# Where VectorE's weight conversions stand among the block products of a two-layer MLP, one Trainium2 core

## The chip, the core and the metric

The kernel runs on one core of a Trainium2 chip. Its time is device microseconds of one execution. TensorE (PE in the rows) multiplies, VectorE (DVE), ScalarE (ACT) and GpSimd (POOL) work on its results, SyncE (SP) issues the transfers. Each engine runs its instructions in the order in which the program lists them: an instruction that waits holds up all that stand behind it on that engine.

## The reference

Clustered attention gives `x` (2 batches, 768 tokens, 512 features). Two MLPs follow:

```python
X = np.fft.fft(np.fft.fft(x, axis=1), axis=2)
u = x + np.real(X)
un = (u - u.mean(-1)) / sqrt(var(u) + 1e-6)
u = u + np.maximum(un @ w_ch1, 0.0) @ w_ch2          # 512 -> 2048 -> 512
h = np.maximum(u @ w_in, 0.0)                        # 512 -> 1024
conv_out = 3-tap convolution of h along the tokens with conv_w
out = (h * sigmoid(conv_out)) @ w_out                # 1024 -> 512
```

The weights come as 64-bit floats. A conversion on the chip makes them 32-bit, and each is then multiplied as two 16-bit parts, high and low.

## The kernel before, in words

Attention comes first, and the change does not touch it. Then the first MLP runs over batch 0 (`g = 0`) and batch 1 (`g = 1`), sixteen blocks of 128 hidden features each (`f`), and after it the second MLP over both batches, eight blocks each.

**The products of a pair.** For batch 1 the up-projection of two blocks `2p` and `2p+1`, called pair p here, is made of seven block products instead of eight, in `ups(p)`. TensorE makes them in the order p1, p6, p2, p7, p5, p4, p3; each is six matmuls of 384 columns. What comes out is added up on VectorE:

- `u1` is a copy of p1 by ScalarE; `u2 = u1 + p6`; `u3 = u2 + p7`;
- `c1` low half `= u1 + p2`; `c2` high half `= u3 + p5`; `c2` low half `= u3 + p4`;
- p5 is also copied by ScalarE, and GpSimd makes `u4 = u2 + p5`; `c1` high half `= u4 + p3`;
- `keep` makes the hidden block from `c2`, then from `c1`: ScalarE the high part (L1754), VectorE the low part (L1755).

Every product lies in one of **two banks** of tag `up`, taken in turn. So TensorE can start a product only when all readers of the product two before it are done. The transposed token tiles and the token scales (`xT`, `cb`, below) take their turn in the same two banks.

**The down-projection between them.** `downs` is a generator: each step is the three matmuls of 512 columns of one token tile, here called a tile. `in_turn` deals products (u) and tiles (d) by a string; a pair has seven products and the twelve tiles of two blocks: `u d u d d u d u d d` in the even block, then `u d d u d d u d d`. After the tiles named in `when`, a step of `side` runs. For batch 1 that is `gate_in(0)`, which prepares batch 0 for the second MLP: two steps that measure tokens, six that turn a token tile (four transposes on TensorE into a bank, then a copy by ScalarE, L1906, and the low part by VectorE, L1907), two that spread the scales (`cb`).

**Sums of weights.** Four of the seven products take sums of weight blocks. `weight_sums(p)` makes them on GpSimd (L1719 to L1723, tile `sv`, one buffer), then splits them: high part by ScalarE (L1726), low part by VectorE (L1727).

**Conversions of the second MLP's weights.** `load_w("b", i)` loads 1 MB into one of two raw buffers and converts it: VectorE L710, L711, L713 (`wb`), ScalarE the square of the low word L712, a check L716, and two sums of squares L759, whose scratch is the raw buffer, so that it is free for the next load only behind them. The eight loads stand in the code behind blocks 1, 3, 5, 7, 9, 10, 11, 12 of batch 1. A scheduler then orders each engine's queue: it may take an instruction from further down in the code when it reckons that it is ready. `tc.issue_after(i)` makes it keep the instructions under it behind `i` on the same engine.

At the end of the stage `scales("b")` adds the sums of squares on TensorE (`sumsb`), and `split_16` splits converted weights (L1681 ScalarE, L1682 VectorE) while the second MLP's first products (`u`, L492) run.

Of the kernel before, what the change touches and what calls it, by code (L numbers as in the profile page):

```python
# [449 lines left out]
def tile_net(ctx, tc, qk, v, cen, w12, w34, conv, dft, odd, out, general):  # L450
# [277 lines left out]
    def load_w(k, f):  # L728
# [15 lines left out]
        with tc.issue_after(last_op[0]) if last_op else nullcontext():  # L744
            ops = from64(w, raw, None if general else sums[:, 64 + f:65 + f])
            for op in ops[0:2] + ops[3:4] if not general else ops:
                i = op()
            last_op[:] = [i.ins]
# [963 lines left out]
    sums_w = {}  # L1712

    def weight_sums(p):
        k = hp.tile([128, 2048], F32, tag="sv", bufs=1, name=f"sv{p}").rearrange("p (s c n) -> p s c n", s=8, c=2)
# [7 lines left out]
        G.tensor_sub(v[:, 3], a1[:, 1], v[:, 1])  # L1723
        t = hp.tile([128, 1024], F32, tag="src", bufs=2, name=f"s16{p}").bitcast(F16)
        t = sums_w[p] = t.rearrange("p (a s c n) -> p a s c n", a=2, s=4, c=2)
        A.copy(t[:, 0], v)  # L1726
        V.tensor_sub(t[:, 1], v, t[:, 0])  # L1727

    def ups(p):
# [30 lines left out]
        A.copy(u1, o)  # L1760
# [5 lines left out]
        V.tensor_add(c1[:, lo], u1, product("p2", own(0, 1), 1))  # L1766
        yield
        u3 = piece("u3")
        V.tensor_add(u3, u2, product("p7", of_sum(2), 5))
        yield  # L1770
        o = product("p5", of_sum(0), 3)
        p5 = piece("p5")
        A.copy(p5, o)
        c2 = row(1)
        V.tensor_add(c2[:, hi], u3, o)
        u4 = piece("u4")
        G.tensor_add(u4, u2, p5)
        yield
        V.tensor_add(c2[:, lo], u3, product("p4", own(1, 1), 6))
        keep(c2, 2 * p)  # L1780
        yield
        V.tensor_add(c1[:, hi], u4, product("p3", of_sum(3), 2))
# [172 lines left out]
    for g in range(B):  # L1955
        for f in range(16):
# [3 lines left out]
            if not general and g == 0 and f > 13:  # L1960
                weight_sums(f - 14)
            if not general and g and f % 2 == 0 and f < 12:
                weight_sums(f // 2 + 2)
            if (g, f) == (B - 1, 15):
                next(side, None)
            steps = downs(0, g, f, side, (1, 4) if g == 0 and f else (2,))
# [3 lines left out]
            elif g == 0:  # L1970
                in_turn(steps, ups(0), iter("ududduuduudud"))
            elif f % 2:
                in_turn(steps, *made)
            else:
                made = (ups(f // 2 + 1), iter("ududdududduddudduddudd")) if f < 14 else ((), repeat("d"))
                in_turn(steps, *made)
            for i in A_LOADS[f] if g == 0 else ():
                load_w("a", i)
# [3 lines left out]
            if g == 1 and f in B_LOADS:  # L1982
                load_w("b", B_LOADS.index(f))
# [14 lines left out]
            for i in {13: (0,), 14: (1,), 15: (2,)}.get(f, ()) if g == 1 else ():  # L1998
                ws_b[i] = split_16(wbp[0], "b", i)
# [3 lines left out]
    for n in range(-3, 8 * B):  # L2003
        if n + 3 < 8 * B:
            mlp2_up((n + 3) // 8, (n + 3) % 8)
        if 0 <= n + 2 < 8 * B:
# [91 lines left out]
```

## Time and profile before

| | us |
|---|---|
| median of 3 runs | 638.51 (636.48 to 639.45) |
| the profiled execution | 637.55 |
| its span, first to last instruction | 635.8 |
| what lies around the span | 1.75 |
| batch 1's products, until the second MLP | 366 to 498 of the span |
| TensorE busy over the span | 602.3 |
| VectorE busy | 509.4 |
| ScalarE busy | 438.2 |
| GpSimd busy | 236.0 |

Busy time is that of instructions; TensorE's matmuls overlap, so what counts for it is when the next one starts. A row's idle time in brackets is the time for which that engine stood still just before it, and the arrow names what ended it.

### The profile page before, as it was taken

How to read it: one execution, taken by the hardware profiler on the slowest of the kernel's cores; microseconds unless marked ns; L12 is line 12 of the kernel's file. 1: busy time of each engine (PE TensorE's matmuls, PEld its weight loads, DVE VectorE, ACT ScalarE, POOL GpSimd, SP SyncE). 2: the span in 40 equal slices, each digit the busy share in tenths (PEclk: the TensorE clock that was granted, in tenths of full speed). 3: DMA queues.
4: the chain of work that ended last, by engine and by line, in shares of the span. 5: the costliest groups of instructions: out<-in, count | busy, mean ns of one | idle time of the engine just before them, and what ended most of it. 6: DMA issues, size and time to landing. Idle time of an engine off the chain costs nothing.

```text
span 635.8 us, 11958 instructions
## 1 busy us (share of the span) xinstructions
PE 602.3 (95%) x4707; PEld 366.7 (58%) x4707; DVE 509.4 (80%) x833; ACT 438.2 (69%) x744; POOL 236.0 (37%) x193
## 2 busy tenths in 40 slices
PE   8899899999999999999999898989999999999995
PEld 4476577676877755566555454544455555555542
DVE  5989979899898898878798298888643799877663
ACT  6788889996889777774678236677511968867652
POOL 4978877875797300001005616445501000000000
PEclk9999999999999999999999999999999999999998
DMA  4776754541310414430432301314200003245202
GB/s 151 206 183 210 210 152 126 155 126 46 100 42 9 195 65 134 142 124 1 147 119 71 129 2 66 133 51 154 96 1 1 1 0 101 101 147 170 81 1 105
DMA packets 21945, 64.41 MB, mean 101 GB/s; under 512 B 7126, under 2 KB 8822, under 8 KB 19064
## 3 DMA queue, kind: packets, MB, share of 16 engines
q1 hardware_dynamic: 20872, 59.81, 29.6%
q0 software_dynamic: 1008, 3.75, 1.9%
q8 instruction: 39, 0.64, 0.4%
q14 instruction: 26, 0.21, 0.1%
HBM read 49.59 MB, written 4.89 MB: 86 GB/s over the span
## 4 chain that ended last, share of the span: by engine, by line
PE 56%; DVE 25%; ACT 12%; issue 3%; DMA 2%; POOL 1%; DVEq 0%; ACTq 0%
PE acc L494 6%; PE acc L493 6%; PE acc L492 6%; PE av L1325 5%; PE t L1269 4%; DVE m6all L1218 4%; PE t L1271 4%; PE s L1209 3%; PE av L1318 2%; PE u L492 2%; PE u L493 2%; PE u L494 2%; PE p L492 2%; DVE wb L711 2%; PE p L493 2%
## 5 line engine op out<-in xcount | busy, mean ns | idle before, releaser
L1306 POOL TENSOR_TENSOR p<-p,p 128x768 f16<-128x768 f32 x61 | 108.1, 1781 | 39.1 <-DVE p L1294 15.0
L1218 DVE TENSOR_REDUCE m6all<-s 128x1 f32<-128x768 f32 x96 | 90.0, 949 | 9.8 <-PE s L1209 7.5
L1278 ACT ACTIVATE p<-t,cbias 128x768 f32<-128x768 f32 x93 | 83.2, 897 | 14.2 <-PE t L1271 13.5
L492 PE MATMUL acc<-wa,h 128*128 128x512 f16 x186 | 70.6, 379 | 0.0
L493 PE MATMUL acc<-wa,h 128*128 128x512 f16 x186 | 70.5, 379 | 0.0
L494 PE MATMUL acc<-wa,h 128*128 128x512 f16 x186 | 70.5, 379 | 0.0
L1325 PEld LDWEIGHTS <-p 128*128 128x128 f16 x1458 | 55.0, 98 | 11.9 <-issue 3.1
L1325 PE MATMUL av<-V,p 128*128 128x65 f16 x1458 | 58.2, 194 | 0.0
L1269 PE MATMUL t<-X 97*128 97x384 f16 x192 | 47.5, 328 | 4.7 <-DVE m6all L1218 2.4
L1209 PE MATMUL s<-X 80*128 80x384 f16 x192 | 46.9, 328 | 5.0 <-DVE eq L1014 3.0
L1296 ACT CAST p<-p 128x768 f16<-128x768 f32 x60 | 49.5, 825 | 0.9
L674 POOL TENSOR_TENSOR rs<-rs,half 128x1 f32<-128x1 f32 x12 | 9.2, 768 | 105.9 <-DVE rs L669 99.7
L1271 PE MATMUL t<-Y 128*128 128x384 f16 x192 | 47.2, 327 | 0.0
L1719 POOL TENSOR_TENSOR sv<-wa 128x512 f32<-128x512 f16 x16 | 26.2, 1657 | 51.7 <-DVE s L1727 37.0
L492 PE MATMUL up<-un,wa 128*128 128x384 f16 x128 | 41.7, 326 | 3.5 <-DVE h L1708 1.9
L492 PE MATMUL u<-x,wb 128*128 128x384 f16 x128 | 41.7, 326 | 1.2 <-DVE h L1803 1.1
L494 PE MATMUL up<-un,wa 128*128 128x384 f16 x128 | 41.7, 326 | 0.0
L493 PE MATMUL up<-un,wa 128*128 128x384 f16 x128 | 41.7, 326 | 0.0
L494 PE MATMUL u<-x,wb 128*128 128x384 f16 x128 | 41.7, 326 | 0.0
L493 PE MATMUL u<-x,wb 128*128 128x384 f16 x128 | 41.7, 326 | 0.0
L493 PE MATMUL acc<-wb,gH 128*128 128x512 f16 x96 | 36.4, 379 | 0.0
L492 PE MATMUL acc<-wb,gH 128*128 128x512 f16 x96 | 36.4, 379 | 0.0
(411 smaller groups left out, 1521.8 us busy)
## 6 DMA issues: line engine op xcount, KB each, us to landing
rawa<-w SPq DMA_DIRECT2D x14, 1024.0 KB
rawb<-w SPq DMA_DIRECT2D x8, 1024.0 KB
heads<-qk SPq DMA_DIRECT2D x8, 768.0 KB
raw<-qk SPq DMA_DIRECT2D x7, 768.0 KB
Y<-G SPq DMA_DIRECT2D x27, 192.0 KB
vraw<-v SPq DMA_DIRECT2D x8, 384.0 KB
heads<-v SPq DMA_DIRECT2D x8, 384.0 KB
out<-y SPq DMA_DIRECT2D x12, 256.0 KB
```

What stands on the lines that cost most here:

```text
L492: T.matmul(o, sH, mH, start=start, stop=False)
L493: T.matmul(o, sH, mL, start=False, stop=False)
L494: T.matmul(o, sL, mH, start=False, stop=stop)
L1209: T.matmul(t[:, c, 0:384], X[0:80, 0, sl], X[0:80, 1, 384 * c:384 * c + 384], start=True, stop=True)
L1218: V.tensor_reduce(m6s[h][:, i:i + 1], t[:, :, 0:384], AX.XY, ALU.max, negate=True)
L1269: T.matmul(t[:, c, 0:384], X[0:rx, 1, sl], X[0:rx, 0, 384 * c:384 * c + 384], start=True, stop=False)
L1271: T.matmul(t[:, c, 0:384], Y[0:ry, k, sl], Y[0:ry, q, 384 * c:384 * c + 384], start=False, stop=True)
L1278: A.activation(p, t[:, :, 0:384], AF.Exp, bias=cbias[:, 0:1], scale=0.125 if general else 0.125 / QK_SCALE ** 2)
L1296: A.copy(p16[:, 0], p32s[n])
L1306: eng.tensor_sub(p16[:, 1], p, p16[:, 0])
L1325: T.matmul(o, p16[:, k, 128 * j:128 * j + 128], v16[:, i, h % 2, 65 * part:65 * part + 65], start=(i + j + k + part == 0), stop=(i == 5), ...
L1719: G.tensor_add(d, w[:, 0, 0], w[:, 1, 0])
```

## The change

- **Conversions.** Each of the three VectorE instructions of a conversion is put behind an addition of the last pair whose addition is in the code by then (`marks`): L710 behind `u3`, L711 behind the high half of `c2`, L713 behind its low half. They can no longer be taken ahead of these.
- **Splits and sums.** Making the sums and splitting them become two functions with their own tables of places (`WEIGHT_SUMS`, `SUM_SPLITS`). The sums are made a step earlier in the code; VectorE's part of each split is put behind the low half of `c1`.
- **One addition moves.** `u2 + p5` is done by VectorE, in place and straight from the bank. GpSimd's addition and ScalarE's copy of p5 go. `u3` now lies in the high half of `c1`.
- **Token tiles** are turned behind tile 5 of an even block and tile 3 of an odd one, instead of behind tile 2 of each.
- Pair 0 (in the last block of batch 0) has another string of u and d; the second MLP's third split (`ws_b[2]`) moves behind its first product block.

```diff
@@ -743,8 +743,13 @@
             return
         with tc.issue_after(last_op[0]) if last_op else nullcontext():
             ops = from64(w, raw, None if general else sums[:, 64 + f:65 + f])
-            for op in ops[0:2] + ops[3:4] if not general else ops:
-                i = op()
+            if general:
+                for op in ops:
+                    i = op()
+            else:
+                for op, m in ((ops[0], "u3"), (ops[1], "c2"), (ops[3], "c2lo")):
+                    with tc.issue_after(marks[m]):
+                        i = op()
             last_op[:] = [i.ins]
         if not general:
             ops[2]()
@@ -1709,10 +1714,12 @@
         if general and g and f < 15:
             ws[0, g, f + 1] = split_16(hp, "a", f + 1)
 
-    sums_w = {}
+    sums_w, marks = {}, {}
+    SUM_SPLITS = {14: (0,), 15: (1,), **{2 * p + 12: (p,) for p in range(2, 8)}}
+    WEIGHT_SUMS = {12: (0,), 14: (1,), 15: (2,), **{2 * p + 10: (p,) for p in range(3, 8)}}
 
     def weight_sums(p):
-        k = hp.tile([128, 2048], F32, tag="sv", bufs=1, name=f"sv{p}").rearrange("p (s c n) -> p s c n", s=8, c=2)
+        k = sums_w[p] = hp.tile([128, 2048], F32, tag="sv", bufs=1, name=f"sv{p}").rearrange("p (s c n) -> p s c n", s=8, c=2)
         v, a1, a2 = k[:, 0:4], k[:, 4:6], k[:, 6:8]
         for f, d in ((2 * p, a2), (2 * p + 1, a1)):
             w = w32["a", f].rearrange("p (a i h c n) -> p a i h c n", a=2, i=2, h=2, c=2)
@@ -1721,10 +1728,15 @@
         G.tensor_sub(v[:, 1], v[:, 0], a1[:, 0])
         G.tensor_sub(v[:, 2], a1[:, 0], a2[:, 0])
         G.tensor_sub(v[:, 3], a1[:, 1], v[:, 1])
+
+    def split_sums(p):
+        v = sums_w[p][:, 0:4]
         t = hp.tile([128, 1024], F32, tag="src", bufs=2, name=f"s16{p}").bitcast(F16)
         t = sums_w[p] = t.rearrange("p (a s c n) -> p a s c n", a=2, s=4, c=2)
-        A.copy(t[:, 0], v)
-        V.tensor_sub(t[:, 1], v, t[:, 0])
+        with tc.issue_after(marks["u1"]) if p == 1 else nullcontext():
+            A.copy(t[:, 0], v)
+        with tc.issue_after(marks["c1"]) if marks else nullcontext():
+            V.tensor_sub(t[:, 1], v, t[:, 0])
 
     def ups(p):
         un, sw = uns[1], sums_w.pop(p)
@@ -1757,29 +1769,26 @@
         lo, hi = slice(0, 384), slice(384, 768)
         o = product("p1", own(0, 0), 0)
         u1 = piece("u1")
-        A.copy(u1, o)
+        marks["u1"] = A.copy(u1, o).ins
         yield
         u2 = piece("u2")
         V.tensor_add(u2, u1, product("p6", of_sum(1), 4))
         yield
         c1 = row(0)
-        V.tensor_add(c1[:, lo], u1, product("p2", own(0, 1), 1))
+        marks["c1"] = V.tensor_add(c1[:, lo], u1, product("p2", own(0, 1), 1)).ins
         yield
-        u3 = piece("u3")
-        V.tensor_add(u3, u2, product("p7", of_sum(2), 5))
+        u3 = c1[:, hi]
+        marks["u3"] = V.tensor_add(u3, u2, product("p7", of_sum(2), 5)).ins
         yield
         o = product("p5", of_sum(0), 3)
-        p5 = piece("p5")
-        A.copy(p5, o)
         c2 = row(1)
-        V.tensor_add(c2[:, hi], u3, o)
-        u4 = piece("u4")
-        G.tensor_add(u4, u2, p5)
+        marks["c2"] = V.tensor_add(c2[:, hi], u3, o).ins
+        V.tensor_add(u2, u2, o)
         yield
-        V.tensor_add(c2[:, lo], u3, product("p4", own(1, 1), 6))
+        marks["c2lo"] = V.tensor_add(c2[:, lo], u3, product("p4", own(1, 1), 6)).ins
         keep(c2, 2 * p)
         yield
-        V.tensor_add(c1[:, hi], u4, product("p3", of_sum(3), 2))
+        V.tensor_add(c1[:, hi], u2, product("p3", of_sum(3), 2))
         keep(c1, 2 * p + 1)
         yield
 
@@ -1957,30 +1966,33 @@
             pairs = not general and (g > 0 or f == 15)
             if (g, f) < (B - 1, 15) and not pairs:
                 mlp1_up(*((g, f + 1) if f < 15 else (g + 1, 0)))
-            if not general and g == 0 and f > 13:
-                weight_sums(f - 14)
-            if not general and g and f % 2 == 0 and f < 12:
-                weight_sums(f // 2 + 2)
             if (g, f) == (B - 1, 15):
                 next(side, None)
-            steps = downs(0, g, f, side, (1, 4) if g == 0 and f else (2,))
+            when = (1, 4) if g == 0 and f else (2,) if general or not g else (3,) if f % 2 else (5,)
+            steps = downs(0, g, f, side, when)
             if not pairs:
                 for _ in steps:
                     pass
             elif g == 0:
-                in_turn(steps, ups(0), iter("ududduuduudud"))
+                in_turn(steps, ups(0), iter("uduududuududd"))
             elif f % 2:
                 in_turn(steps, *made)
             else:
                 made = (ups(f // 2 + 1), iter("ududdududduddudduddudd")) if f < 14 else ((), repeat("d"))
                 in_turn(steps, *made)
+            for p in SUM_SPLITS.get(16 * g + f, ()) if not general else ():
+                split_sums(p)
+            for p in WEIGHT_SUMS.get(16 * g + f, ()) if not general else ():
+                weight_sums(p)
             for i in A_LOADS[f] if g == 0 else ():
                 load_w("a", i)
             if g == 0 and f in (13, 14):
                 raw = cvs[0].tile([128, 2048], I32, tag="raw64", bufs=2, name=f"junk{f}")
                 squares("a", f - 13, raw[:, 0:256].bitcast(BF16))
             if g == 1 and f in B_LOADS:
-                load_w("b", B_LOADS.index(f))
+                for i in range(8):
+                    if B_LOADS[i] == f:
+                        load_w("b", i)
             if (g, f) == (0, 14):
                 scales("a")
             if (g, f) == (0, 15):
@@ -1995,7 +2007,7 @@
                 V.tensor_scalar(cw, cw, scl["b"][:, 6:7], None, ALU.mult)
                 out_scale(0)
                 A.activation(warm, scl["b"][:, 0:1], AF.Sigmoid)
-            for i in {13: (0,), 14: (1,), 15: (2,)}.get(f, ()) if g == 1 else ():
+            for i in {13: (0,), 14: (1,), 15: (2,) if general else ()}.get(f, ()) if g == 1 else ():
                 ws_b[i] = split_16(wbp[0], "b", i)
     hctx.close()
     gps.append(pool(ctx, "gp", side="right"))
@@ -2003,6 +2015,8 @@
     for n in range(-3, 8 * B):
         if n + 3 < 8 * B:
             mlp2_up((n + 3) // 8, (n + 3) % 8)
+        if n == -3 and not general:
+            ws_b[2] = split_16(wbp[0], "b", 2)
         if 0 <= n + 2 < 8 * B:
             gate((n + 2) // 8, (n + 2) % 8)
         if n < 0:
```

VectorE in pair 2, from the third addition on. The digits behind a tile's name are the pair and the half or the block (`uc20` is `c1` of pair 2, `uc21` is `c2`, `p52` is p5 of pair 2, `xT01` the second token tile turned, `wb2` the third converted weight block). Before:

```order
L1769 TENSOR_TENSOR u32_5505<-u22_5464,p72_5506 128x384
L710 TENSOR_SCALAR wb2_5744<-rawb2_5745 128x1024
L711 SCALAR_TENSOR_TENSOR wb2_5744<-rawb2_5745,wb2_5744 128x1024
L1775 TENSOR_TENSOR uc21_5529<-u32_5505,p52_5520 128x384
L713 SCALAR_TENSOR_TENSOR wb2_5744<-rawb2_5745,wb2_5744 128x1024
L1779 TENSOR_TENSOR uc21_5529<-u32_5505,p42_5539 128x384
L1755 SCALAR_TENSOR_TENSOR h1_4_5547<-uc21_5529,h1_4_5547 128x768
L1907 TENSOR_TENSOR x0_5338<-xT01_5560,x0_5338 128x4x128
L1782 TENSOR_TENSOR uc20_5493<-u42_5531,p32_5570 128x384
L710 TENSOR_SCALAR wb3_5887<-rawb3_5888 128x1024
```

With the change:

```order
L1781 TENSOR_TENSOR uc20_5468<-u22_5453,p72_5480 128x384
L710 TENSOR_SCALAR wb1_5582<-rawb1_5583 128x1024
L1916 TENSOR_TENSOR x0_5357<-xT00_5501,x0_5357 128x4x128
L1785 TENSOR_TENSOR uc21_5525<-uc20_5468,p52_5518 128x384
L1786 TENSOR_TENSOR u22_5453<-u22_5453,p52_5518 128x384
L711 SCALAR_TENSOR_TENSOR wb1_5582<-rawb1_5583,wb1_5582 128x1024
L1788 TENSOR_TENSOR uc21_5525<-uc20_5468,p42_5534 128x384
L713 SCALAR_TENSOR_TENSOR wb1_5582<-rawb1_5583,wb1_5582 128x1024
L1767 SCALAR_TENSOR_TENSOR h1_4_5542<-uc21_5525,h1_4_5542 128x768
L1791 TENSOR_TENSOR uc20_5468<-u22_5453,p32_5565 128x384
L1916 TENSOR_TENSOR x0_5357<-xT01_5558,x0_5357 128x4x128
L1767 SCALAR_TENSOR_TENSOR h1_5_5573<-uc20_5468,h1_5_5573 128x768
```

The conversion in this pair is now block 1 instead of block 2. L711 moved from ahead of the addition of p5 to behind two of them, L713 from ahead of the addition of p4 to behind it, and the low part of the turned tile (line 1907 before, 1916 now) from ahead of the addition of p3 to behind it.

ScalarE in the odd block of pair 3, from the square of the low word on. Before:

```order
L712 ACTIVATE rawb4_6030<-rawb4_6030 128x1024
L716 ACTIVATE rawb4_6030,sums_3937<-rawb4_6030 128x1024
L1754 ACTIVATE h1_6_5702<-uc31_5684 128x768
L1906 CAST x0_5338<-xT03_5715 128x4
L759 ACTIVATE rawb4_6030,sums_3937<-wb4_6029 128x512
L712 ACTIVATE craw_6039<-craw_6039 128x24
L759 ACTIVATE rawb4_6030,sums_3937<-wb4_6029 128x512
L1906 CAST x0_5338<-xT03_5715 128x4x127
L1726 CAST s165_5761<-sv5_5754 128x1024
L1754 ACTIVATE h1_7_5735<-uc30_5648 128x768
```

With the change:

```order
L712 ACTIVATE rawb2_5736<-rawb2_5736 128x1024
L1766 ACTIVATE h1_6_5693<-uc31_5676 128x768
L716 ACTIVATE rawb2_5736,sums_3937<-rawb2_5736 128x1024
L1915 CAST x0_5357<-xT03_5709 128x4
L1737 CAST s165_5806<-sv5_5662 128x1024
L1915 CAST x0_5357<-xT03_5709 128x4x127
L1766 ACTIVATE h1_7_5726<-uc30_5619 128x768
L764 ACTIVATE rawb2_5736,sums_3937<-wb2_5735 128x512
```

The copies of the turned tile `xT03` stood ahead of the split of the sums `s165`; now that split stands between them, and the check L716 stands ahead of both.

VectorE at the end of batch 0, where blocks 13 and 14 leave their hidden parts `h0_13` and `h0_14`. Before:

```order
L1708 SCALAR_TENSOR_TENSOR h0_13_4987<-up0_13_1_5003,h0_13_4987 128x384
L1727 TENSOR_TENSOR s160_5152<-sv0_5145,s160_5152 128x1024
L1708 SCALAR_TENSOR_TENSOR h0_14_5049<-up0_14_0_5050,h0_14_5049 128x384
L1727 TENSOR_TENSOR s161_5197<-sv1_5190,s161_5197 128x1024
L1708 SCALAR_TENSOR_TENSOR h0_14_5049<-up0_14_1_5065,h0_14_5049 128x384
```

With the change:

```order
L1713 SCALAR_TENSOR_TENSOR h0_13_4987<-up0_13_1_5003,h0_13_4987 128x384
L1739 TENSOR_TENSOR s160_5170<-sv0_5036,s160_5170 128x1024
L1713 SCALAR_TENSOR_TENSOR h0_14_5056<-up0_14_0_5057,h0_14_5056 128x384
L1713 SCALAR_TENSOR_TENSOR h0_14_5056<-up0_14_1_5072,h0_14_5056 128x384
L1713 SCALAR_TENSOR_TENSOR h0_15_5121<-up0_15_0_5122,h0_15_5121 128x384
```

The split of pair 1's sums, `s161`, no longer stands between the two halves of `h0_14`; it now stands in pair 0, behind the addition of p2.

## Rows read from the trace of the kernel before

**Rows 1.** Busy time by stretch: TensorE, weight loads, VectorE, ScalarE, GpSimd, clock, transfers.

```profile
391.00:456.00 65.00, 58.10 (x318) 31.25 (x317) 54.44 (x67) 42.79 (x81) 36.40 (x28) 1.00 0.33 117
504.00:620.00 116.00, 115.84 (x635) 61.58 (x634) 91.52 (x172) 81.22 (x149) 0.00 (x0) 1.00 0.25 82
```

**Rows 2.** TensorE's waits, 349 to 505: us in total, times, longest.

```profile
PE p L492 <- DVE u L1763: 4.5, 3, 1.8
PE p L492 <- DVE x L1907: 2.4, 3, 1.5
PE up L492 <- DVE h L1708: 1.9, 1, 1.9
PE u L492 <- DVE h L1803: 1.1, 1, 1.1
```

**Rows 3.** TensorE in order of time: start, us, instruction, idle time ahead.

```profile
394.67 0.60 PE L1904 MATMUL xT<-ident,U 128*128 128x128 f32 x4
397.06 0.32 PE L492 MATMUL p<-un,wa 128*128 128x384 f16 x1 [1.79 <-DVE u L1763]
...
460.27 0.33 PE L492 MATMUL p<-un,wa 128*128 128x384 f16 x1
...
461.89 0.33 PE L492 MATMUL p<-un,s 128*128 128x384 f16 x1
...
464.16 0.33 PE L492 MATMUL p<-un,wa 128*128 128x384 f16 x1
```

**Rows 4.** VectorE in order of time, pairs 2 and 4.

```profile
394.36 2.18 DVE L711 SCALAR_TENSOR_TENSOR wb<-rawb,wb 128x1024 int32<-128x1024 int32 x1
396.46 0.54 DVE L1763 TENSOR_TENSOR u<-u,p 128x384 f32<-128x384 f32 x1
396.93 1.71 DVE L713 SCALAR_TENSOR_TENSOR wb<-rawb,wb 128x1024 uint32<-128x1024 uint32 x1
...
402.49 1.23 DVE L711 SCALAR_TENSOR_TENSOR wb<-rawb,wb 128x1024 int32<-128x1024 int32 x1
...
407.92 0.68 DVE L1907 TENSOR_TENSOR x<-xT,x 128x512 f16<-128x512 f32 x1
...
431.16 2.06 DVE L711 SCALAR_TENSOR_TENSOR wb<-rawb,wb 128x1024 int32<-128x1024 int32 x1
```

**Rows 5.** ScalarE in order of time, odd block of pair 2.

```profile
403.75 1.17 ACT L712 ACTIVATE rawb<-rawb 128x1024 f32<-128x1024 f32 x1 [0.48 <-DVE wb L711]
404.94 1.18 ACT L716 ACTIVATE rawb<-rawb 128x1024 f32<-128x1024 f32 x1
...
406.17 0.84 ACT L1754 ACTIVATE h<-uc 128x768 f16<-128x768 f32 x1
406.92 0.57 ACT L1906 CAST x<-xT 128x512 f16<-128x512 f32 x1
...
408.77 1.03 ACT L1726 CAST s<-sv 128x1024 f16<-128x1024 f32 x1
```

**Rows 6.** GpSimd in order of time, sums of pairs 1 and 4.

```profile
350.85 2.26 POOL L1719 TENSOR_TENSOR sv<-wa 128x512 f32<-128x512 f16 x2 [4.18 <-DVE s L1727]
...
397.51 1.72 POOL L1720 TENSOR_TENSOR sv<-sv 128x256 f32<-128x256 f32 x1
399.19 0.72 POOL L1722 TENSOR_TENSOR sv<-sv 128x256 f32<-128x256 f32 x1
```

**Rows 7.** VectorE in order of time, end of batch 0.

```profile
357.07 1.23 DVE L1727 TENSOR_TENSOR s<-sv,s 128x1024 f16<-128x1024 f32 x1 [5.21 <-ACT s L1726]
```

**Rows 8.** VectorE in order of time, start of the second MLP.

```profile
497.26 3.67 DVE L1849 SCALAR_TENSOR_TENSOR U<-acc,U 128x512 f32<-128x512 f32 x6
500.86 1.40 DVE L1682 SCALAR_TENSOR_TENSOR wb<-wb,scb,wb 128x512 f16<-128x512 f32 x2
502.19 0.55 DVE L1809 SCALAR_TENSOR_TENSOR h<-u,x 128x384 f32<-128x384 f32 x1
```

**Rows 9.** The chain that ended last, where a load of raw weights stands in it.

```profile
425.68 4.73 DMA rawb<-w
```

## The prediction

> **What bounds the kernel now.** I first cut the span into stretches [rows 1]. From 504 to 620 us TensorE stands still for 0.2 us, so whatever the change does to VectorE or ScalarE there is covered by TensorE, and time won earlier arrives at the end in full. It stands still before that, 6.9 us in the middle of batch 1 (391 to 456). TensorE's waits name the causes [rows 2]: 4.5 us for `u2` and 2.4 for turned token tiles (both keep one of the two banks occupied), which are those 6.9; 1.9 for a hidden part `h` at the end of batch 0; 1.1 for the second MLP's `h`. VectorE is busy for 54 of the 65 us of batch 1's middle, so it is its order rather than its load that TensorE meets.
>
> A wait costs a little more than its idle time. A matmul's row is 0.33 long, but six of them, a product, take 0.975 (below), 0.16 each: the next starts before the last has drained. In [rows 3] the transposes at 394.67, 0.60 long, so hold TensorE for 0.44; the product should start at 395.11 and starts at 397.06, 1.95 later, for a row that shows 1.79 idle. I add 0.16 per wait. **What is to be won**: batch 1 six waits, 6.9 + 6 x 0.16 = 7.8; batch 0's end 2.1; second MLP 1.3; 11.2 us in all.
>
> **The unit of the working.** A product and one tile take 1.62 us on TensorE, a product and two tiles 2.27 [rows 3]: a tile 0.645, a product 0.975. From the start of a pair (p1) they follow at these distances when nothing waits.
>
> **Batch 0's end.** VectorE waited 5.21 us for ScalarE's part of `s161` [rows 7]; the second half of `h0_14` stood behind it, and TensorE for that one. With the change `s161` stands in pair 0 behind the addition of p2, by when its sums are long made. Is something late there instead? p2 ends 3.6 us into pair 0 (its string has p1, tile, p6, p2), is added by 4.4, the split takes 1.23 [rows 7] to 5.5, one add of an accumulator 0.6 (six in 3.67, [rows 8]), and the third addition, 0.55, ends at 6.6. p4 takes its bank at 6.8 (after tile, p7, tile, p5). It fits by 0.2. **Won: 2.1.**
>
> **Additions.** VectorE gets one more addition per pair, start to start 0.47 (396.46 to 396.93, [rows 4]), 3.8 us over eight pairs, on an engine with 11 us free in the stretch. ScalarE's copies and GpSimd's additions go; no wait of TensorE is for either, so that is worth nothing by itself.
>
> **The six old waits go.** They came about as follows. The first conversion's L711 ran ahead of `u2` (394.36 to 396.5, [rows 4]), and the turned tile, turned between p6 and p2, took the bank that p7 needs 1.6 us later. With the change no conversion stands ahead of `u2`, and the even block's tile is turned behind p7. Its bank is wanted by p4, behind p5 and two tiles, 2.27 later; 0.25 until the end is noticed (0.16 for the last matmul to drain, 0.1 for the hand-over, my estimate), copy 0.57 [rows 5], low part 0.68 [rows 4]: 1.5. **Won: 7.8.** But other things are late next.
>
> **The new wait: the odd block's turned tile, wanted by the next pair's p1.** It is now turned one tile later (2.27 instead of 2.9 us ahead of p1), and its copy on ScalarE stands behind the square L712, the hidden part, and the check L716. L712 cannot start before L711 has read the raw words, and L711 now waits for the addition of p5. From the end of p5 (zero) in pairs 2 and 4:
>
> - VectorE's first addition of p5 starts at 0.48: it stands behind the low part of the even tile, which ends 0.56 after p5 (turned just ahead of it, -0.975 + 0.25 + 0.57 + 0.68, hand-overs 0.04);
> - two additions, 0.47 each: L711 starts at 1.42;
> - L711: 1.23 where GpSimd stands still, 2.18 and 2.06 where it runs [rows 4]. GpSimd starts its sums when the split is done, 2.0 after p2's end (0.26 to notice, 0.47, 1.23); L711 comes 5.75 after it (tile, p7, two tiles, transposes, p5, 1.42). GpSimd needs 5.1 alone (2.26 and four of 0.72, [rows 6]), so they meet. I take **2.06**, the row of pair 4, where the short later additions of the sums ran beside it, as they will here: 3.48;
> - ScalarE, start to start: L712 1.19, L716 1.23, hidden part 0.75, then the copy 0.57; VectorE's low part 0.68; hand-overs 0.1 [rows 4, 5]: 4.5 more, 8.0;
> - TensorE wants p1 after two tiles, p4, two tiles, the transposes, p3, two tiles: 1.29 + 0.975 + 1.29 + 0.44 + 0.975 + 1.29 = 6.26.
>
> TensorE loses 1.7 in each of these two pairs. In pair 3 the split of `s165`, 1.03 [rows 5], stands between the two copies of `xT03`: 2.8. In pair 5 the bank holds token scales, which ScalarE copies ahead of L716: 8.0 becomes about 6.2, no wait. Pairs 6 and 7 turn nothing. Sum 6.2. Bounds: L711 at 1.23 gives 0.9 + 1.9 + 0.9 = 3.7; at 2.18, 6.6.
>
> **Smaller ones.** `u1` stands on ScalarE behind the same L712, hidden part, L716, a split, a hidden part and a sum of squares: L711's end + 6.2. At the start of pair 2, where no turned tile has held TensorE up, p2 wants it 5.5 after L711's end if L711 starts, behind the last token measures, at 10.9 of pair 1; I put 0.7 (0 with a short L711). At pair 6 the same sum gives 0.1. p3 wants its bank at 4.0 after p5 and the addition of p4 ends by 4.1: 0.05 each, 0.1 in all. The load of block 6 lands 4.73 after its issue [rows 9], the raw buffer being free 4.8 into pair 6: at 9.6, wanted at 11.2. Block 7's at 3.5 of pair 7, wanted at 7.2. New waits in batch 1: **7.1** (3.7 to 7.6).
>
> **Second MLP.** One of two low parts that stood ahead of the first `h` (1.40 for two, [rows 8]) moves behind it: TensorE's 1.3 becomes 0.6; some of it comes back at the fourth half, which now stands behind two convolution steps. **Won: 0.5** (0 to 0.7).
>
> **Sum.** 2.1 + 7.8 - 7.1 + 0.5 = 3.3 us (2.3 to 6.9 by the bounds: 7.6 lost and nothing won in the second MLP, or 3.7 and 0.7): 637.55 becomes 634.2. The profiled execution is 0.96 below the median of the three runs; the mean of all four times is 638.0, and I forecast 638.0 - 3.3 = **634.7**. A measurement of this kernel tells about 0.5%, 3.2 us, from no change, and that lies right at the forecast.
>
> **A rule weighed.** GpSimd's L1720 took 1.72 beside VectorE's L713 and its like 0.72 right behind it [rows 4, 6]; L713 took 1.71. Both engines slow down. The Trainium skill (SBUF — State Buffer, section "Who interferes with whom") says that an instruction of VectorE with two SBUF inputs and one of GpSimd that reads SBUF exclude each other, and that whoever starts first keeps the port for its whole instruction. By that rule the new waits would be those of rival 2 below.
>
> **Rivals.**
>
> 1. *L711 and GpSimd miss each other.* Then 3.7 is lost instead of 7.1, 6.7 won: 631.3. For it: L711 took 1.23 in the odd block of pair 2 [rows 4]. Against: GpSimd stood still there, and will not now. Chance 0.15.
> 2. *L711 waits for one short addition of GpSimd and then runs undisturbed.* That is at most 0.72 + 1.23 = 1.95, about 1.6 on the mean: the three waits become 1.3 + 2.3 + 1.3, the smaller ones 0.4, and 5.1 is won: 632.9. Against: 2.06 and 2.18 [rows 4] lie above its most. This is the rule just named. Chance 0.12.
> 3. *The old waits only change their names, and batch 0's end too.* `s161` fits into pair 0 by 0.2 only; if the accumulators' adds come a little otherwise, p4 waits there and the 2.1 shrinks; a wait of some 0.2 per pair at p3, which fits as narrowly, takes the rest: 1 won, 637. Chance 0.17.
> 4. *Slower: the last conversion comes late.* Block 7, converted between pairs 4 and 5 before, is now converted in the last pair, and on ScalarE its squares stand ahead of the hidden part that the very next tile needs; there nothing is to spare. Its load waits for block 5's squares, and VectorE for the load. The slack is 3.7 us (3.5 against 7.2); beyond that each us of delay costs TensorE one. Slower by 0.5% needs 3.7 + 3.3 + 3.2 = 10 us of delay, a load of 14.7 instead of 4.73 [rows 9]; at 11 us: 642. Against: no other load is under way then but block 6's. Chance 0.06.
>
> The forecast (1.5 to 5 us won, 633 to 636.5) has 0.50.
>
> **How the numbers follow.** Half of the forecast's chance and all of rivals 1 and 2 lie beyond 0.5%: faster 0.25 + 0.15 + 0.12 = 0.52. The other half and rival 3: same 0.42. Rival 4: slower 0.06. The range leaves out rival 4 and what lies beyond rival 1 (no wait at all at the turned tiles), and takes in rival 3 with the scatter of the runs: 630.5 to 638.4.
>
> **What would show it.** Right: no wait of TensorE for `h` near 356; none for `u2` in pairs 2 to 5; instead three waits at the first product of pairs 3, 4, 5, released by VectorE's low part of a turned tile, near 1.7, 2.8 and 1.7 us; L711 near 2 us in the odd blocks; the second MLP's wait near 0.6. Wrong: those three waits gone or under 1 us with L711 near 1.2 (rivals 1 and 2); a wait in pair 0 (rival 3); TensorE standing at `sumsb` or at the first tile of block 14 (rival 4).

## The result, and the profile after

The changed kernel took 628.64 us (median of 4 runs, 628.1 to 629.34), the kernel before 637.69 beside it: ratio 0.9857, 95% interval 0.9828 to 0.9885. That is 9.05 us less and faster by more than the 0.5% that a measurement tells; forecast were 634.7 and a range down to 630.5. Measured once more beside other kernels it had 629.69, ratio 0.9848 (0.983 to 0.9865). The profiled execution took 628.88 with a span of 627.1, so 8.7 of span are to be explained.

TensorE by stretch in the changed kernel, columns as in [rows 1]: the end of batch 0, the pairs 2 to 5 of batch 1, the second MLP's start, and the rest.

```profile
349.00:364.00 15.00, 15.00 (x85) 8.18 (x83) 4.16 (x12) 3.40 (x9) 5.04 (x6) 1.00 0.38 141
...
389.00:452.00 63.00, 62.53 (x346) 33.64 (x344) 48.90 (x65) 31.83 (x63) 30.45 (x25) 1.00 0.20 68
490.00:498.00 8.00, 7.33 (x46) 4.30 (x45) 6.20 (x15) 7.24 (x13) 0.00 (x0) 1.00 0.01 2
498.00:612.00 114.00, 113.42 (x620) 60.09 (x618) 90.34 (x171) 79.42 (x145) 0.00 (x0) 1.00 0.26 84
```

Where TensorE stood still for 6.9 of 65 us in batch 1's middle, it now does for 0.5 of 63. Its waits from 340 to 505, which answer to [rows 2]:

```profile
PE u L492 <- DVE h L1818: 0.7, 1, 0.7
PE acc L494 <- DVE h L1767: 0.3, 1, 0.3
PE acc L492 <- ACT gH L1836: 0.2, 1, 0.2
```

The waits for `u2`, for turned tiles and for `h` of batch 0 are gone, as forecast. The three waits at p1 of pairs 3, 4 and 5, forecast at 6.2 us in all, are missing too: they are not in this list at all. VectorE's rows around p1 of pair 3 and of pair 4 show what p1 does start behind (L1791 is the addition of p3, which ends `c1`; L1916 the turned tile's low part; line numbers in a run's rows are those of its own kernel):

```profile
399.55 1.50 DVE L711 SCALAR_TENSOR_TENSOR wb<-rawb,wb 128x1024 int32<-128x1024 int32 x1
...
404.05 0.54 DVE L1791 TENSOR_TENSOR uc<-u,p 128x384 f32<-128x384 f32 x1
404.62 0.69 DVE L1916 TENSOR_TENSOR x<-xT,x 128x512 f16<-128x512 f32 x1
...
415.21 1.43 DVE L711 SCALAR_TENSOR_TENSOR wb<-rawb,wb 128x1024 int32<-128x1024 int32 x1
...
419.65 0.54 DVE L1791 TENSOR_TENSOR uc<-u,p 128x384 f32<-128x384 f32 x1
...
421.23 0.69 DVE L1916 TENSOR_TENSOR x<-xT,x 128x508 f16<-128x508 f32 x1 [0.95 <-ACT x L1915]
```

and TensorE, the first matmuls of p1 in pairs 3 and 4 and of p6 in pair 4:

```profile
404.64 0.32 PE L492 MATMUL p<-un,wa 128*128 128x384 f16 x1
...
420.25 0.32 PE L492 MATMUL p<-un,wa 128*128 128x384 f16 x1
...
421.97 0.34 PE L492 MATMUL p<-un,s 128*128 128x384 f16 x1
```

p1 starts 0.05 and 0.06 us behind the end of L1791 (404.59, 420.19), long before the tile's low part is done. In pair 4 it is p6 that starts 0.05 behind the low part's end (421.92). So p1 has p3's bank, and the turned tile's bank went to p6, which needs it a product and a tile later. The compiled program says the same; the bank of the second turned tile of a pair, of p3, and of the next pair's p1 and p6 (`xT01`, `p32` and `p13` are those of pairs 2, 2 and 3):

```
before  xT01:1 p32:0 p13:1 p63:0   xT03:0 p33:1 p14:1 p64:0   xT05:0 p34:1 p15:0 p65:1
after   xT01:0 p32:1 p13:1 p63:0   xT03:0 p33:1 p14:1 p64:0   xT05:0 p34:1 p15:1 p65:0
```

The banks are not taken in turn, as the description of the kernel and the prediction have it. In the kernel before, too, p33 and p14 had the same one.

The second number that came out otherwise is L711, taken as 2.06: it is 1.50 and 1.43 here.

### The profile page after: what moved, and what is told of

It reads as the page before. It is cut to its first block, busy times and chain, and to the rows that moved or that the text cites. A ratio compares the mean times of both kernels' runs of the same rounds, so it can differ in the third digit from the quotient of the medians.

```text
span 627.1 us, 11926 instructions
## 1 busy us (share of the span) xinstructions
PE 601.3 (96%) x4707; PEld 366.5 (58%) x4707; DVE 512.2 (82%) x841; ACT 432.6 (69%) x736; POOL 226.2 (36%) x185
## 4 chain that ended last, share of the span: by engine, by line
PE 63%; DVE 21%; ACT 9%; issue 3%; DMA 2%; POOL 1%; DVEq 0%; ACTq 0%
PE acc L494 6%; PE acc L493 6%; PE acc L492 6%; PE av L1330 5%; PE t L1274 4%; DVE m6all L1223 4%; PE t L1276 4%; PE s L1214 3%; PE av L1323 2%; PE u L492 2%; PE u L494 2%; PE u L493 2%; PE p L492 2%; PE p L494 2%; PE p L493 2%
## 5 line engine op out<-in xcount | busy, mean ns | idle before, releaser
L1726 POOL TENSOR_TENSOR sv<-wa 128x512 f32<-128x512 f16 x16 | 21.7, 1377 | 70.5 <-DVE s L1739 55.8
```

The source lines that it names most:

```text
L1726: G.tensor_add(d, w[:, 0, 0], w[:, 1, 0])
```

## The experiments

Ratios are to the kernel before, measured beside each, with their 95% intervals. These are 0.16 to 0.29% wide to either side, 1.0 to 1.8 us, so a difference between the medians of two versions is no surer than that; the losses of TensorE in the traces are the finer measure.

**1. The banks strictly in turn** (`e1_strict_turn`).

```diff
-        return bank("up", 2, name)
+        turn.append(name)
+        return bank(("upA", "upB")[len(turn) % 2], 1, name)
```

> The changed kernel with its two product banks handed out strictly in turn in the order of the code (bank A, bank B, A, ...), all else as it is. Theory A (the predicted wait is missing because the first product p1 of pairs 3, 4 and 5 takes the bank of p3, whose last reader is VectorE's addition L1791, and not the bank of the turned tile): p1 now takes the turned tile's bank and starts when the tile's low part ends, which in the changed kernel's trace ends at 405.31, 421.92 and 436.70, against p1's starts at 404.64, 420.25 and 436.03: waits of about 0.9, 1.9 and 0.9 us at p1 instead of 0.2 each, 3.1 us more in all, 631.7 us (631 to 632.5). Theory B (the banks were in turn already and p1's wait shrank because L711 took 1.46 instead of 2.06): no change, 628.6, and p1's waits stay at 0.2.

631.57 us, 0.9898 (0.988 to 0.9917). TensorE's waits, and the rows of the three p1 with the last matmul ahead of the second:

```profile
PE p L492 <- DVE x L1919: 1.7, 3, 0.6
```

```profile
404.80 0.34 PE L492 MATMUL p<-un,wa 128*128 128x384 f16 x1 [0.55 <-DVE x L1919]
...
421.03 0.33 PE L494 MATMUL p<-un,s 128*128 128x384 f16 x1
421.99 0.34 PE L492 MATMUL p<-un,wa 128*128 128x384 f16 x1 [0.63 <-DVE x L1919]
...
437.26 0.34 PE L492 MATMUL p<-un,wa 128*128 128x384 f16 x1 [0.55 <-DVE x L1919]
```

The forecast wait is there once the banks are in turn. By the distance of matmul starts TensorE loses 0.71, 0.80 and 0.70, against 0.19, 0.14 and 0.20 in the changed kernel: 1.7 us more. In pair 4 the scheduler has put a tile and three matmuls of p6 (the row at 421.03 is the last, on `s`) ahead of p1, 1.13 us of work; in pairs 3 and 5 it has put one matmul of the next tile there, 0.22 each. Without that the three losses would be 0.93, 1.93 and 0.92, the 0.9, 1.9 and 0.9 expected. Theory A holds. (The medians lie 2.9 apart; the traced execution was the fastest of this experiment.)

**2. Only the order on VectorE changed** (`e1b_low_first`).

```diff
+        with tc.issue_after(marks["x"]) if 2 <= p < 5 else nullcontext():
             V.tensor_add(c1[:, hi], u2, product("p3", of_sum(3), 2))
```

(`marks["x"]` is the last low part of a turned tile.)

> The changed kernel with one more order on VectorE: in pairs 2, 3 and 4 the addition of p3 (L1791) stands behind the low part of the odd block's turned tile, not ahead of it. The bank code is untouched. Theory A (a product takes the bank that is released first in the order of the instructions): the turned tile's bank is now released first, so p1 takes it and waits for the low part, about 0.9, 1.9 and 0.9 us as with the banks in turn, about 3 us more: 631.7 (631 to 633). Theory B (p1 and p6 have fixed banks): p1 still waits for the addition, which now ends 0.5 behind the low part: 0.5 more at each, 1.2, 2.4 and 1.2, with p6 nowhere late: 633.5.

630.98 us, 0.988 (0.9863 to 0.9896). The program's banks became `xT01:0 p32:1 p13:0`, `xT03:1 p33:0 p14:1`, `xT05:0 p34:1 p15:0`: p1 now has the tile's bank each time. Its waits:

```profile
PE p L492 <- DVE x L1917: 1.8, 3, 0.7
```

By the distance of matmul starts TensorE loses 0.68, 0.84 and 0.72, the same as with the banks in turn. In these pairs p1 gets the bank whose last reader stands first in the order of instructions, and that order is what the section on the change prints: L1907 moved from ahead of the addition of p3 to behind it. The kernel before agrees: its p13 and p15 had the tile's bank, with L1907 ahead of the addition, and its p14 had p33's, with the last L1907 of that tile behind it (426.43 after 425.57).

**3. The conversions let go again** (`e4_conv_early`).

```diff
-                for op, m in ((ops[0], "u3"), (ops[1], "c2"), (ops[3], "c2lo")):
-                    with tc.issue_after(marks[m]):
-                        i = op()
+                for op in ops[0:2] + ops[3:4]:
+                    i = op()
```

> The changed kernel without the three marks that place the conversions' L710, L711 and L713 behind the additions of p7, p5 and p4; everything else as it is. In the order that results L711 (1.2 to 2.2 us) stands ahead of the low part of the even block's turned tile and of the additions of p5 in pairs 2 and 3, and L713 ahead of the sums u2 in pairs 2 and 3. Theory A (the marks carry part of the gain): p4 waits for the turned tile's bank and p7 for u2, 0.3 to 0.7 us in each of pairs 2 to 4, about 2 us: 630.6 (629.3 to 632.5). Rival (turning the token tiles elsewhere and taking the addition from GpSimd carry it all): 628.6, no wait above 0.3.

635.11 us, 0.9951 (0.9935 to 0.9968): 6.5 more than the changed kernel, three times what was expected.

```profile
PE p L492 <- DVE x L1915: 4.2, 5, 1.5
...
PE p L492 <- DVE u L1785: 0.5, 1, 0.5
PE p L492 <- DVE u L1774: 0.3, 1, 0.3
```

A conversion stands ahead of the even tile's low part again, L711 in pairs 2 and 3, L713 and the next block's L710 in pair 4. p4 waits for that bank for 1.0, 0.85 and 1.5 us; the other 0.9 of the 4.2 is p1, for the odd tile.

**4. The end of batch 0 as before** (`e7_s161_early`): sums and splits of pairs 0 and 1 made ahead of blocks 14 and 15 again, without marks.

```diff
+            if not general and g == 0 and f > 13:
+                weight_sums(f - 14)
+                split_sums(f - 14)
```

> The changed kernel with the sums of pairs 0 and 1 made and split where the kernel before had them, in the last two blocks of batch 0 and in the order that the scheduler gives; pairs 2 to 7 as changed. Theory (2.1 us of the gain is the end of batch 0): VectorE waits again for ScalarE's part of the split of pair 1, the hidden part of block 14 stands behind it, and TensorE stands still for about 1.9 us near 356: 630.7 (630 to 631.5). Rival (with GpSimd and ScalarE freed elsewhere the split comes in time): 628.6, no wait near 356.

630.57 us, 0.9868 (0.9852 to 0.9885), a span of 629.0 against 627.1, with the old wait back:

```profile
PE up L492 <- DVE h L1713: 1.9, 1, 1.9
```

**5. GpSimd's first long addition three times** (`e8_turn_long_sums`), on top of experiment 1.

```diff
-        for f, d in ((2 * p, a2), (2 * p + 1, a1)):
+        for f, d in ((2 * p, a2),) * (3 if p > 2 else 1) + ((2 * p + 1, a1),):
```

> The kernel with the banks strictly in turn, and GpSimd makes the first long addition (L1729 here, 128x512 of 16-bit weights) of each of pairs 3 to 7 three times, the same result each time, so that L711 of blocks 1 to 3 now meets a long addition and not the short ones. Theory (L711 waits for the one GpSimd instruction under way and then runs its 1.23 undisturbed; in the kernel before it met the long additions, which made 2.06 and 2.18, in the changed kernel the short ones, which made 1.46): L711 becomes 1.8 (1.3 to 2.4), the turned tile's low part comes that much later, and p1 of pairs 3 to 5 waits 0.3 to 0.6 longer each than with the banks in turn alone: 1 to 1.8 us more than there, 632.5 to 633.3. Rival (L711's length is set by where VectorE stands, not by GpSimd): L711 stays at 1.46 and nothing changes, 631.5.

639.62 us, 1.0009 (0.9989 to 1.0029). The longer L711 that was aimed at did not come: it took 1.72, 1.25 and 1.22 in the three blocks, where 1.8 was expected, for it met a short addition in the first and a long one just before its end in the other two. But each time it ended 1.08 us after the end of the addition that it met (406.32 after 405.24, 422.24 after 421.16, 442.53 after 441.45), as the theory has it and as in the other runs, below. The time says nothing of L711: the sums came so late that ScalarE's part of a split waited 2.58 us for them, `u1` stood behind it, and TensorE waited 1.98 for `u1`. In pair 3 the split waited 2.52, between the two copies of `xT03`, and p1 of pair 4 waited 2.98 for that tile.

**6. Token tiles turned at the old places** (`e3_when2`).

```diff
-            when = (1, 4) if g == 0 and f else (2,) if general or not g else (3,) if f % 2 else (5,)
+            when = (1, 4) if g == 0 and f else (2,)
```

> The changed kernel with the token tiles of batch 1's pairs turned where the kernel before turned them, behind the third tile of every block; conversions, splits, sums and additions as changed. Theory A (the tiles' place matters little once no conversion stands ahead of u2: the low part then follows u2 at once and ends about 1.5 us after its tile, against 1.62 until p7 wants the bank): 629.1 (628.4 to 630), waits at p7 below 0.3 each. Theory B (the tiles had to be moved; with the old places p7 waits for the low part as before, 0.6 to 1.6 in each of pairs 2 to 4): 631 to 632.

628.44 us, 0.9849 (0.9828 to 0.9871), waits for turned tiles:

```profile
PE p L492 <- DVE x L1916: 0.4, 2, 0.2
```

p7 waits in no pair: the two waits are at p1 of pairs 3 and 5, for the odd block's tile, 0.34 and 0.35 lost. Moving the tiles brought nothing that these runs can tell.

**7. GpSimd's addition again** (`e5_gpsimd_add`).

```diff
-        V.tensor_add(u2, u2, o)
+        p5 = piece("p5")
+        A.copy(p5, o)
+        G.tensor_add(u2, u2, p5)
```

> The changed kernel with the addition u2 + p5 made by GpSimd again, from a copy of p5 that ScalarE makes; all else as changed. Theory A (worth nothing by itself, as the prediction had it, for VectorE has time): 628.6 (628 to 629.3). Theory B (GpSimd is busy with the next pair's sums from 1.9 us after p2's end for 7.4 us, so the addition for p3 comes late and p3's bank with it): waits of 0.5 to 2 us at the products behind p3 in pairs 2 to 5, 630.5 to 634.

632.94 us, 0.9917 (0.9891 to 0.9943): 4.3 more than the changed kernel. The addition stands behind the sums on GpSimd; in pair 1, GpSimd, then VectorE:

```profile
389.85 0.72 POOL L1730 TENSOR_TENSOR sv<-sv 128x256 f32<-128x256 f32 x1
390.54 1.71 POOL L1788 TENSOR_TENSOR u<-u,p 128x384 f32<-128x384 f32 x1
```

```profile
392.28 0.56 DVE L1793 TENSOR_TENSOR uc<-u,p 128x384 f32<-128x384 f32 x1 [0.89 <-POOL u L1788]
```

The addition of p3 waits for it, and TensorE for the bank of p3 (1.05 of this in pair 1). With that addition late, the low part of the turned tile stands ahead of it on VectorE in pairs 2 and 4, and p1 of pairs 3 and 5 waits for the tile's bank:

```profile
PE p L492 <- DVE uc L1793: 2.5, 3, 1.0
PE p L492 <- DVE x L1918: 1.8, 2, 0.9
```

**8. Two more instructions moved** (`e9_later`): L713 of the first conversion behind the last hidden part of pair 1, and both low parts of `ws_b[2]` behind the first `h2`.

```diff
-                for op, m in ((ops[0], "u3"), (ops[1], "c2"), (ops[3], "c2lo")):
+                for op, m in ((ops[0], "u3"), (ops[1], "c2"), (ops[3], "c2lo" if f else "h")):
...
-            ws_b[2] = split_16(wbp[0], "b", 2)
+            with tc.issue_after(marks["h2"]):
+                ws_b[2] = split_16(wbp[0], "b", 2)
```

> The changed kernel with two more instructions moved: L713 of the first conversion behind the last hidden part of pair 1 (TensorE waits 0.48 + 0.25 us there in the changed kernel), and both low parts of the second MLP's block 2 behind the first h2 (TensorE waits 0.84 there). Theory A (both waits go): 627.3 (626.8 to 628.2), with no wait above 0.3 at the first tile of pair 2 and near 492. Rival (they come back one step later, at u2 of pair 2 behind L713 and at the third half product): 628.6, waits of the same size beside the old places.

626.95 us, 0.9821 (0.9804 to 0.9839). The waits aimed at are gone; 0.3 came back at a later half product:

```profile
PE u L492 <- DVE h L1812: 0.3, 1, 0.3
```

Then single parts, put into the kernel before.

**9. The conversions' places alone** (`f1_marks_alone`): the marks at the additions and the loop over them, from the change's diff, nothing else.

> The kernel before with one part of the change alone: the conversions' L710, L711 and L713 stand behind the additions of p7, p5 and p4 of their pair. Theory A (the conversions' place and VectorE's addition only work together: with GpSimd's addition the sum for p3 stands behind the next pair's sums, as in the run that gave the addition back to GpSimd, which lost 4.3): no wait for u2 any more, but 0.7 to 1.2 us at the products behind p3 in pairs 1 to 5: 634 to 636.5. Rival (the six old waits, 7.8, go with the conversions alone, as the prediction's working has it): 630.5 to 631.5.

630.8 us, 0.9876 (0.9854 to 0.9898), span 629.1, 6.7 less than before. Theory A was wrong, the rival right: the old waits (7.8) go with this part alone, but for 0.6 lost at one `u2` and 0.2, 0.1 and 0.2 at three p1, 1.1 in all; with sums and splits where the old scheduler puts them, GpSimd's addition is not late.

**10. VectorE's addition alone** (`f2_vadd_alone`): `V.tensor_add(u2, u2, o)` in place of copy and GpSimd's addition, with `u3` in the high half of `c1` as in the change.

> The kernel before with another part alone: VectorE adds p5 to u2 itself, no copy by ScalarE and no addition by GpSimd. Theory A (worth nothing by itself, since L711 still stands ahead of u2): waits for u2 of 1 to 2 us in pairs 2 and 4 stay; 636.5 to 639. Rival (GpSimd's late addition was among what held the pairs up in the kernel before): 633 to 635.

645.52 us, 1.0096 (1.0073 to 1.0119): slower by 6, which neither theory had. TensorE waits longer for `u2`, because L710 (394.91, 1.65 long) now runs behind the hidden part too and both it and L711 (396.59, 2.05) stand between that part and `u2`; in the kernel before L710 ran at 391.38 and took 0.69. Behind the wait the clock falls. Waits, then stretches (the clock is the third number from the end):

```profile
PE p L492 <- DVE u L1763: 7.5, 3, 3.1
```

```profile
396.00:399.00 3.00, 0.08 (x1) 0.00 (x0) 2.97 (x3) 0.32 (x1) 3.00 (x3) 1.00 0.01 3
400.00:403.00 3.00, 3.00 (x9) 1.22 (x8) 1.47 (x3) 2.88 (x7) 2.32 (x3) 0.50 0.00 0
404.00:410.00 6.00, 6.00 (x35) 3.31 (x33) 4.86 (x7) 3.02 (x5) 0.00 (x0) 1.00 0.43 168
```

There are three such stretches, one behind each wait for `u2`. By the distance of matmul starts they cost 1.7, 1.6 and 1.7 us, 5.0 of the 7.5 that TensorE loses more in this trace than in that of the kernel before; the waits for `u2` themselves are 3.0 longer.

**11. Both** (`f3_marks_vadd`).

> The kernel before with these two parts together and nothing else: conversions behind the additions, and VectorE's addition of p5. Theory A (these two carry the whole middle of batch 1; left are the end of batch 0, 2.1, and the second MLP, 0.5): 631 (630 to 632), no wait above 0.5 in pairs 2 to 5, the 1.9 near 356 still there. Rival (the tiles' new places or the new places of the splits are needed as well): 633 or more.

629.26 us, 0.9848 (0.9832 to 0.9864), with two waits left from 340 to 505, both outside batch 1's middle:

```profile
PE up L492 <- DVE h L1713: 1.9, 1, 1.9
PE u L492 <- DVE h L1805: 1.3, 1, 1.3
```

The span is 627.9, 1.2 less than in experiment 9. The two intervals overlap, so the addition's own share is seen in the traces alone.

**12. The changed kernel again** (`e10_again`).

> The changed kernel once more, beside the others on the same chip: 628.6 (628 to 629.5), ratio 0.9857 as before; the version with two more instructions moved had 0.9821, and if that is a gain the two intervals should part or the ratio here stay above 0.984.

629.69 us (627.72 to 632.23), 0.9848 (0.983 to 0.9865). Its interval overlaps that of experiment 8, so whether 626.95 is a gain over the changed kernel stays open.

**13. Three parts, and four** (`g1_three_parts`, `g2_four_parts`): experiment 11 with the split of pair 1's sums moved into pair 0 and pair 0's new string; then also the low parts of `ws_b[2]` as in experiment 8.

```diff
-                in_turn(steps, ups(0), iter("ududduuduudud"))
+                in_turn(steps, ups(0), iter("uduududuududd"))
+                with tc.issue_after(marks["u1"]), tc.issue_after(marks["c1"]):
+                    split_sums(*late.pop())
```

> The kernel before with three parts of the change: conversions behind the additions, VectorE's addition of p5, and the split of pair 1's sums moved into pair 0 (with the changed kernel's order of pair 0). Tiles, the other splits and sums and the second MLP as before. Theory A (the parts add up: 9.7 for the first two, 2.1 for the end of batch 0, and what is left out brought nothing): 627.2 (626.3 to 628.3), no wait near 356, none above 0.5 in batch 1, 1.5 in the second MLP. Rival (the split of pair 1 comes late in pair 0 when the other splits stay where they were): a wait of 0.5 to 2 us in pair 0 or 1, 628.5 to 630.

> The same with both low parts of the second MLP's block 2 behind the first h2 as well. Theory A (TensorE's 1.5 near the start of the second MLP becomes 0.2 to 0.6): 626.2 (625.3 to 627.2), below the changed kernel's 628.6 and level with or below the 626.95 of the version with two more instructions moved. Rival (the wait only moves to the third half): 627.2.

628.15 us, 0.9839 (0.9813 to 0.9864), and 627.34 us, 0.9828 (0.9804 to 0.9852). In the first TensorE's waits from 340 to 505 are

```profile
PE u L492 <- DVE h L1813: 1.4, 1, 1.4
PE p L492 <- DVE u L1776: 0.2, 1, 0.2
```

The places of the other splits and of the tiles were not needed: three parts reach the time of the whole change. The fourth takes the 1.4 down to 0.3, and its time does not part from the others.

**L711 across the runs.** GpSimd, then VectorE, in the kernel before (pair 4; its L711 at 431.16 is in [rows 4]), in experiment 6 and in experiment 3:

```profile
428.68 3.46 POOL L1719 TENSOR_TENSOR sv<-wa 128x512 f32<-128x512 f16 x2 [6.61 <-DVE s L1727]
```

```profile
397.95 0.72 POOL L1727 TENSOR_TENSOR sv<-sv 128x256 f32<-128x256 f32 x1
398.64 1.71 POOL L1729 TENSOR_TENSOR sv<-sv 128x256 f32<-128x256 f32 x1
```

```profile
398.01 1.75 DVE L711 SCALAR_TENSOR_TENSOR wb<-rawb,wb 128x1024 int32<-128x1024 int32 x1
```

```profile
396.97 2.71 POOL L1725 TENSOR_TENSOR sv<-wa 128x512 f32<-128x512 f16 x2 [7.72 <-DVE s L1738]
```

```profile
398.71 2.06 DVE L711 SCALAR_TENSOR_TENSOR wb<-rawb,wb 128x1024 int32<-128x1024 int32 x1
```

L711 ends 1.08 to 1.09 us after the end of the GpSimd addition that was under way when it started: 433.22 after 432.14, 399.76 after 398.67, 400.77 after 399.68. In the changed kernel, whose GpSimd had

```profile
399.24 0.72 POOL L1729 TENSOR_TENSOR sv<-sv 128x256 f32<-128x256 f32 x1
399.93 1.71 POOL L1728 TENSOR_TENSOR sv<-sv 128x256 f32<-128x256 f32 x1
```

beside the L711 at 399.55, it is 1.09 (401.05 after 399.96), and in the runs where GpSimd stood still L711 took 1.22. So it waits for one instruction of GpSimd and then runs undisturbed; the next GpSimd instruction waits for it in turn (1.71 for one of 0.72). That is the rule of the Trainium skill (SBUF — State Buffer, section "Who interferes with whom"). The trace agrees but for 0.14: after the wait L711 takes 1.08, not the whole 1.22 that it takes alone; what of it runs during the wait no run here shows.

## Why the prediction was wrong

**The step that failed** is "The new wait: the odd block's turned tile, wanted by the next pair's p1": 6.2 us forecast, 0.19 + 0.14 + 0.20 = 0.5 measured. Of the 5.7 missing:

- 1.7 is the false premise that the banks are taken in turn. Experiment 1 made the premise true, and the three losses rose from 0.5 to 2.2; experiment 2 did the same by the order of two VectorE instructions. Without the work that the scheduler moved there (below) the premise would be worth 3.2.
- 1.7 is L711, three times 2.06 less 1.49 (experiment 1's mean). The prediction put the 2.06 down to the "short later additions"; the row at 428.68 shows that it met a long one, which ended 0.98 after L711's start. In the changed kernel it meets short ones.
- 1.6 is the work that the scheduler moved ahead of p1 in experiment 1: a tile and a half product in pair 4, one matmul each in pairs 3 and 5.
- The rest, 0.7, is in the links of the chain, some 0.24 a pair. The copies and checks on ScalarE did stand in the forecast order, but L712 and L716 take 1.08 and 1.13 from start to start in experiment 1, not 1.19 and 1.23, and L711 starts 0.04 sooner after p5. ScalarE in its pair 2:

```profile
400.51 1.19 ACT L712 ACTIVATE rawb<-rawb 128x1024 f32<-128x1024 f32 x1 [3.10 <-DVE wb L711]
401.59 0.83 ACT L1769 ACTIVATE h<-uc 128x768 f16<-128x768 f32 x1
402.33 1.14 ACT L716 ACTIVATE rawb<-rawb 128x1024 f32<-128x1024 f32 x1
...
403.46 0.56 ACT L1918 CAST x<-xT 128x512 f16<-128x512 f32 x1
```

So even with the banks in turn 6.2 would have been 2.2 (3.8 without the moved work). With the banks as they are the tile's chain holds up only p6 of pair 4, by 0.1.

**Right, in size too.** The stretches and what bounds them. Batch 0's end: 2.1 forecast; the stretch 349 to 364 is full, and undoing that part cost 1.9 of span. The six old waits of batch 1: 7.8 forecast, all gone, and the conversions' places alone gave 6.7 of span with 1.1 of new losses.

**Right effect, wrong cause.** The prediction let the old waits go for two reasons, the conversions and the tiles' new places. Experiments 6 and 9 show that the second was not needed: with no conversion ahead of it, the low part of the even tile at the old place holds up no p7.

**Additions "worth nothing by itself"** fell in both directions: VectorE's addition costs 6 in the old order (experiment 10), the greater part through the clock, and giving it back to GpSimd costs 4.3 in the new (experiment 7). TensorE's waits name only the last link, and neither engine was one before.

**Smaller terms.** The 0.7 at the start of pair 2 came at another place: not p2 for `u1`, but the first tile for the hidden part behind L713 (0.48) and the product after it (0.25); experiment 8 moved L713 and both went. That its size is right is luck. In the second MLP 1.3 became 0.84 + 0.24, 0.2 won instead of 0.5.

**The sum as measured**: 2.1 + 7.8 - 0.5 - 0.7 + 0.2 = 8.9, against 8.7 between the spans. It leaves out gaps of under 0.4: a new one of 0.3 for `gH`, and 0.6 of the kernel before that are gone.

**The rivals.** Rival 2 had L711's mechanism right, and the reason given against it was the misread row; its time, 632.9, still had the banks in turn. Of rivals 3 and 4 nothing came. What did come, no wait for the tiles at p1, the prediction names and leaves out of its range without a reason: its chances add up to 1 without it.

## What to carry to other kernels

Before a wait is forecast for a shared buffer, look up in the order of instructions which of its earlier users is released first: which buffer the next user gets follows from that, not from whose turn it is. An instruction of VectorE that may collide with GpSimd is priced by the end of the one it will meet plus its own undisturbed time (here 1.08 of 1.22), not by a row in which it met another. Undo parts singly and also do them alone: here the single undoings cost 6.5, 4.3, 1.9 and 0, 12.7 in all for a gain of 9, and only the parts done alone and together showed that three reach it, most of it through the conversions' places.

## What the runs showed of the hardware that was not expected

After TensorE had stood for 3.08 us in experiment 10, the granted clock was 0.50 from 400 to 403, the lower of its two levels (1.2 GHz), and 1.00 again after that: three microseconds of work that take 1.5 at the full level. It fell in the same way behind that run's waits of 2.19 and 2.25, and behind the 1.98 and 2.98 of experiment 5; behind that experiment's wait of 1.26 it did not. The kernel before had waits of 1.79 and 1.93 with the clock at 1.00 behind them, so its stalls cost only themselves. Stretches behind the 1.98 of experiment 5, then behind the 1.79 of the kernel before:

```profile
397.00:400.00 3.00, 3.00 (x11) 1.26 (x9) 1.69 (x2) 0.42 (x1) 0.62 (x1) 0.52 0.64 218
```

```profile
397.00:400.00 3.00, 2.49 (x14) 1.32 (x14) 2.70 (x4) 2.97 (x6) 3.00 (x4) 1.00 0.00 0
400.00:403.00 3.00, 3.00 (x18) 1.54 (x17) 1.76 (x3) 1.00 (x4) 1.33 (x2) 1.00 0.39 74
```
